# New order of issue in a fused attention and max-out FFN kernel: values and weights ahead of other loads, FFN units between attention steps

## The chip, the cores and the metric

The kernel runs on one core of a Trainium2 chip. The metric is device time in microseconds of one execution; lower is better. Five engines work side by side, each strictly in the order of its own instructions: TensorE (PE, with its weight loads PEld), VectorE (DVE), ScalarE (ACT), GpSimd (POOL) and SyncE (SP), which only issues transfers here. Sixteen DMA engines move the data; transfers issued by SP and ACT go through hardware queues, those issued by POOL, which also turn fp32 into fp16 on the way, through a software queue.

## The reference

Four batches, eight heads, 768 tokens, 64 numbers per head. Heads 0, 2 and 6 look at all earlier tokens, the others ("streaming") only at 4 first tokens and the last 64. The attention's output, 3072 rows of 512, goes through an FFN whose hidden layer is the maximum of three products.

```python
scores = scale * np.matmul(q, k.transpose(0, 1, 3, 2))
stream_keep = causal & (is_sink | in_win)
mask = np.where(retr[0, :, 0, 0, None, None], full_mask, stream_mask)
scores = np.where(mask[None, :, :, :], scores, -1000000000.0)
scores = scores - np.max(scores, axis=-1, keepdims=True)
a = np.exp(scores)
a = a / (np.sum(a, axis=-1, keepdims=True) + 1e-09)
attn = np.matmul(a, v)
x = np.ascontiguousarray(attn.transpose(0, 2, 1, 3)).reshape(B * S, H * D)
h = np.maximum(np.maximum(x @ w1, x @ w2), x @ w3)
return (h @ w_out).astype(np.float32)
```

Shapes: q, k, v are 4 x 8 x 768 x 64, w1 to w3 512 x 768, w_out 768 x 512, all fp32; the result is 3072 x 512 fp32. The kernel works in fp16 with sums in fp32.

## The kernel before

The function `fast` defines some forty small steps and runs them in the order of the list `PROGRAM` (line 83; the loop over it is at line 854). Each item is a step's name, its numbers and, where one applies, a letter for the engine (d DVE with copy, r DVE with a reduction as copy, a ACT, p POOL, s SP's queue). Nothing reorders afterwards: the list alone says what each engine and each queue does first, and an engine whose next instruction waits holds all behind it.

Work is cut by batch (0 to 3) and by half (tokens 0 to 383 and 384 to 767). Batch 0 is treated apart, since it must start at once: its q and k come pair of heads by pair of heads, are cast and turned on PE; later batches come whole by POOL's queue in fp16 and are turned on DVE. The steps that matter here:

- `hl half pair n` (`load_pairs`, line 206): SP loads k and q of batch 0, 192 KB for two heads. `cast`, `turnp`: cast to fp16 and turned by three PE transposes each for k and q. `kx0`: the far keys of streaming heads are copied out.
- `load_v b half` (line 292): SP loads the values, 768 KB a half; for batch 0 with 768-byte runs (three rows of 64 floats), for later batches in three parts with 256-byte runs. `vc half h0 n` casts four heads of them, `vt half blocks` (`sort_v`, line 507) sorts them by PE into rows, `y` and `v` fill the tables of values, `vx` and `va`, that attention reads.
- `load b quad which` (line 248): POOL issues k and q of a later batch, 768 KB of fp16 together, in runs of 24 rows of a head (3072 bytes). `turn` is a DVE transpose of a quarter; `kx` copies far keys.
- `w 0`, `w 1`, `w 2` (line 392): POOL issues a weight, 768 KB of fp16 in runs of 1536 bytes; `w 3` is w_out.
- `s0 half u pair` (line 589): scores of batch 0 and their exponential on ACT; `k0` the masks. `s b step` and `k` the same for later batches. Scores lie in two PSUM tiles (`sps`).
- `av b half hp` (line 711): attention times values for two heads, and DVE's division; its result `x` is turned by PE (`x b half hp`) or, with the letter D, by a transposing DMA from SP.
- `f b half wi ni` (`hidden`, line 449): a unit of the FFN, four matmuls of 384 columns with weight wi and block ni; wi 0 is copied out, 1 and 2 are folded in by DVE as a maximum. There are 18 units to a half; they and the outputs use four PSUM banks (`bkp`). `o b half tb`: an output tile of 128 rows, six matmuls of 512 columns, copied and written by SP.
- `gs wi` (`gate`, line 282): a two-element DMA from SP that reads a weight; SP's next transfer is issued only when that weight has landed. `gp` does the same on POOL for a pair of batch 0. `idle n`: n matmuls on zeros.

A staging tile of `hl` exists twice (`pairs2`), one of values three times (`stage`), so the third `hl` of the pairs waits for the casts of the first.

Of the kernel before, what the change touches and what calls it, by code (L numbers as in the profile page):

```python
# [96 lines left out]
    "turn 1 0 0 1, turn 1 0 1 0, turn 1 1 0 0, kx 1 0 p, y 0 1 5:8:2 r a, f 0 0 0 3 a, s0 1 1 3",
    "s0 1 1 2, f 0 0 0 0 a, f 0 0 0 4 a, f 0 0 0 5 a, f 0 0 0 2 a, gs 0, s0 1 0 2, turn 1 1 1 1",
    "turn 1 1 1 0, s0 1 2 2, f 0 0 0 1 a, y 0 1 4:5:1 r a, k0 1 1 2 p, turn 1 1 0 1",
    "k0 3 1 2 d, av 0 1 0 D, k0 2 0 1 d, av 0 1 1 D, k0 2 1 0 p, k0 2 0 0 p, s 1 1, k 1 1 X 0 d",  # L100
    "k0 2 1 1 p, k 1 1 X 1 d, av 0 1 2 D, load 2 0 0, f 0 0 1 4, f 0 0 1 5, f 0 0 1 3, s 1 0",
    "av 0 1 3, f 0 0 1 2, k 1 0 Y 0 d, f 0 0 1 0, kx 1 1 d, f 0 0 1 1, f 0 0 2 1, s 1 2",
    "k 1 2 Y 0 p, f 0 0 2 2, x 0 1 3 d, f 0 0 2 0, f 0 0 2 4, f 0 1 0 4 a, f 0 1 1 4, f 0 0 2 3",
    "turn 2 0 0 1, s 1 3, f 0 1 0 2 d, k 1 2 X 0 p, f 0 0 2 5, load_v 1 0 s, v 1 0 3 a",
    "turn 2 0 0 0, f 0 1 1 2, flags, w 3, load 2 0 1, k 1 2 X 1 d, y 1 0 1:8:2 r p, f 0 1 2 2, f 0 1 0 0 a, s 1 5",
    "y 1 0 4:5:1 s p, y 1 0 4:5:1 r p, f 0 1 1 0, f 0 1 2 0, y 1 0 1:8:2 s a, f 0 1 0 1 d, s 1 7",
    "f 0 1 0 3 d, k 1 1 Y 0 p, k 1 0 X 0 p, load_v 1 1 s, v 1 1 2 d",
    "k 1 0 X 1 d, v 1 0 1 p, f 0 1 1 1, f 0 1 2 1, f 0 1 2 4, f 0 1 1 3",
# [944 lines left out]
```

## Time and profile before

| | us |
|---|---|
| median of 3 runs | 190.82 |
| lowest, highest | 190.44, 192.43 |
| the profiled execution, its whole time | 190.84 |
| its span, first to last instruction | 189.3 |
| PE busy in the span | 178.8 |
| DVE, ACT, POOL busy | 139.4, 101.2, 82.7 |

The mean granted clock of TensorE over the span is 0.994. Matmuls overlap in the records, so a busy PE is not PE at its peak; idle time of an engine matters only where another engine or the end of the run waits for it. "Busy" in the line of DMA shares counts packets of all queues, so it can pass 1. A wait for several semaphores is put down to the one that came last. HBM was read for 25.17 MB, which is every input once, and written for 6.29 MB, the result.

### The profile page before, as it was taken

The numbers are of one execution on the slowest core, as the hardware profiler recorded it, in microseconds if no ns is written. First come the engines' busy times: TensorE is split into PE (matmuls) and PEld (weight loads), VectorE is DVE, ScalarE is ACT, GpSimd is POOL, SyncE is SP. The second block draws the span as 40 slices with busy tenths as digits, with TensorE's granted clock in tenths as the row PEclk, the third lists the DMA queues.
The fourth block names the chain that finished last, engine by engine and source line by source line (L and its number), as shares of the span: only waits on it lengthen the run. The fifth ranks groups of instructions, "written<-read, shape, count | busy, mean of one in ns | idle before, by whom it ended". The sixth has DMA issues, their size and how long they took to land.

```text
span 189.3 us, 4743 instructions
## 1 busy us (share of the span) xinstructions
PE 178.8 (94%) x1854; PEld 105.0 (55%) x1854; DVE 139.4 (74%) x297; ACT 101.2 (53%) x163; POOL 82.7 (44%) x146
## 2 busy tenths in 40 slices
PE   6888889899999999999999999999999999999990
PEld 2444545666556456755566455856665567455540
DVE  4366999986979999785889976874855768537721
ACT  4579989745695542957438556464555420331020
POOL 7775799704899961125953680205144000000000
PEclk9999999999999999999999999999999999999997
DMA  4999999999899999969989321131122032421043
GB/s 125 313 325 290 214 212 198 170 126 201 150 146 171 161 234 196 259 89 178 283 135 213 78 94 55 24 66 55 21 57 68 0 112 44 115 108 47 0 167 119
DMA packets 44105, 26.60 MB, mean 140 GB/s; under 512 B 31022, under 2 KB 39470, under 8 KB 44078
## 3 DMA queue, kind: packets, MB, share of 16 engines
q1 hardware_dynamic: 39614, 18.19, 40.3%
q0 software_dynamic: 4192, 7.87, 24.4%
q8 instruction: 15, 0.25, 0.5%
q10 hardware_dynamic: 272, 0.20, 0.3%
q14 instruction: 12, 0.10, 0.2%
HBM read 25.17 MB, written 6.29 MB: 166 GB/s over the span
## 4 chain that ended last, share of the span: by engine, by line
PE 79%; DMA 9%; POOL 5%; issue 2%; SPq 2%; DVE 1%; ACT 0%; ACTq 0%; POOLq 0%
PE yy L442 45%; PE yy L472 15%; PE st L682 7%; PE oacc L725 7%; DMA vs<-in_v_dram 6%; POOL pt L378 4%; PE yst L442 3%; DMA qs<-in_q_dram 2%; SPq L206 2%; PE yst L472 1%; POOL vn L505 1%; DVE kx L566 0%; POOL kx L578 0%; POOL qn L220 0%; POOL vx L532 0%
## 5 line engine op out<-in xcount | busy, mean ns | idle before, releaser
L378 POOL TENSOR_TENSOR pt<-pt,kb 128x256 f16<-128x256 f16 (+4 forms) x49 | 42.1, 883 | 43.6 <-ACT pt L699 43.2
L699 ACT ACTIVATE pt<-st 128x1024 f16<-128x1024 f32 (+2 forms) x51 | 43.5, 909 | 31.1 <-PE st L682 31.0
L442 PE MATMUL yy<-xT,w2t 128*128 128x384 f16 x180 | 36.0, 326 | 0.0
L442 PE MATMUL yy<-xT,w0t 128*128 128x384 f16 x184 | 35.0, 326 | 0.0
L442 PE MATMUL yy<-xT,w1t 128*128 128x384 f16 x176 | 34.7, 326 | 0.0
L472 PE MATMUL yy<-woutt,hT 128*128 128x512 f16 (+1 forms) x138 | 31.9, 372 | 0.0
L459 DVE TENSOR_TENSOR acc<-yy,acc 128x384 f16<-128x384 f32 x44 | 24.2, 554 | 9.7 <-PE yy L442 6.7
L459 DVE TENSOR_TENSOR hT<-yy,acc 128x384 f16<-128x384 f32 x45 | 24.8, 556 | 4.7 <-PE yy L442 2.8
L274 DVE STREAM_TRANSPOSE KQ<-kq 128x384 f32<-128x384 f32 x24 | 25.3, 1131 | 0.0
L442 PEld LDWEIGHTS <-w1t 128*128 128x128 f16 x192 | 18.1, 98 | 12.3 <-issue 0.4
L442 PEld LDWEIGHTS <-w0t 128*128 128x128 f16 x192 | 17.8, 98 | 12.8 <-issue 1.1
L442 PEld LDWEIGHTS <-w2t 128*128 128x128 f16 x192 | 17.9, 98 | 11.8 <-issue 0.2
L481 ACT COPY ot<-yy 128x512 f32<-128x512 f32 (+1 forms) x17 | 9.7, 568 | 26.9 <-PE yy L472 24.1
L455 ACT CAST acc<-yy 128x384 f16<-128x384 f32 x31 | 14.6, 491 | 17.1 <-PE yy L442 14.6
L472 PEld LDWEIGHTS <-hT 128*128 128x128 f16 x150 | 14.4, 98 | 14.9
L725 PEld LDWEIGHTS <-pt 128*128 128x128 f16 x472 | 17.0, 97 | 4.3 <-POOL pt L378 1.0
L725 PE MATMUL oacc<-va,pt 128*128 128x65 f16 x392 | 18.8, 193 | 0.0
L732 DVE TENSOR_TENSOR x<-oacc,sums 128x384 f16<-128x384 f32 x32 | 17.8, 557 | 1.1
L378 DVE TENSOR_TENSOR pt<-pt,kb 128x512 f16<-128x512 f16 (+5 forms) x35 | 15.1, 444 | 3.2 <-ACT pt L699 3.1
L637 ACT ACTIVATE pt<-st 128x1024 f16<-128x1024 f32 (+5 forms) x22 | 15.4, 760 | 1.2 <-PE st L616 1.2
L682 PE MATMUL st<-KQ 32*128 32x128 f16 (+2 forms) x342 | 14.9, 257 | 0.0
L725 PE MATMUL oacc<-vx,pt 128*128 128x65 f16 x80 | 11.9, 192 | 0.7 <-POOL pt L378 0.7
(115 smaller groups left out, 184.4 us busy)
## 6 DMA issues: line engine op xcount, KB each, us to landing
out_dram<-ot SPq DMA_DIRECT2D x24, 256.0 KB, 3.0
vs<-in_v_dram SPq DMA_DIRECT2D x18, 256.0 KB, 5.5
ks<-in_k_dram SPq DMA_DIRECT2D x8, 192.0 KB, 5.3
qs<-in_q_dram SPq DMA_DIRECT2D x7, 192.0 KB, 4.5
kq<-in_k_dram POOLq DMA_DIRECT2D x3, 384.0 KB, 6.3
kq<-in_q_dram POOLq DMA_DIRECT2D x3, 384.0 KB, 9.1
kq<-in_k_dram POOLq DMA_DIRECT2D x3, 288.0 KB, 4.8
kq<-in_q_dram POOLq DMA_DIRECT2D x3, 288.0 KB, 6.3
```

The source lines that it names most:

```text
L274: nc.vector.transpose(out=dst.rearrange("c (p j) -> c j p", j=n)[:, j0:j1], in_=src.rearrange("c (j i) -> c j i", i=R),)
L378: engine.tensor_tensor(out=x, in0=x, in1=of_blocks(kb, pattern, rows), op=ALU.mult)
L442: nc.tensor.matmul(begun_units[b, half, wi, ni][:, 0:HALF], w_t[wi][:, ks, ni * P : (ni + 1) * P], xT[b, half, ks].rearrange("p a t -> p ( ...
L455: op(out=acc[b, half, ni], in_=yy[:, 0:HALF])
L459: nc.vector.tensor_tensor(out=acc[b, half, ni] if wi == 1 else hT[b, half, ni], in0=yy[:, 0:HALF], in1=acc[b, half, ni], op=ALU.max,)
L472: nc.tensor.matmul(yo[:, 0:n], hT[b, half, ns][:, tb * P : (tb + 1) * P], woutt[:, ns, c : c + n], start=(ns == 0), stop=(ns == NNB - 1),)
L481: op(out=ot[:, c : c + n], in_=yo[:, 0:n])
L637: nc.scalar.activation(out=pts[0, half, hp, u][:, r0:r1, c0:c1], in_=sts[hp][:, r0:r1, c0:c1], func=AF.Exp, scale=sc,)
L682: nc.tensor.matmul(sts["XY"[g // 2]][:, g % 2, c0 : c0 + n * P], KQ[rows, 0, ki * P : (ki + 1) * P] if kind == "p" else kx[b % 2][quad][ro ...
L699: nc.scalar.activation(out=pts[b, s, xy][:, r0:r1, c0:c1], in_=st[:, r0:r1, c0:c1], func=AF.Exp, scale=sc,)
L725: nc.tensor.matmul(o[:, i, r, 0 : D + 1], at[b, h, kind, ki, qi], vv[:, 0 : D + 1], start=(n == 0), stop=(n == len(todo) - 1), skip_group_ ...
L732: nc.vector.tensor_tensor(out=x, in0=o[:, :, :, 0:D], in1=rc.unsqueeze(3).to_broadcast([P, HB, 2, D]), op=ALU.mult,)
```

## The change

The list `PROGRAM` is replaced as a whole. Apart from three single `idle 1` items that are dropped, and the engine letters of many copies and masks, it holds the same items; all functions are the same.

- SP's queue: the values of half 0 (`load_v 0 0`) come right behind half 0's q and k, ahead of `hl 1 0 2` and `hl 1 2 2`. The values of half 1 (`load_v 0 1`), which had no gate, come behind `gs 0`, with the transposes of half 1's x behind them. Then `load_v 1 0`, the three outputs of half 0, `load_v 2 0` and `load_v 1 1`.
- POOL's queue: `w 0`, `w 1`, `w 2`, then `load 1 0`, `w 3`, `load 1 1`; before it was `load 1 0`, `w 0`, `load 1 1`, `w 1`, `w 2`, and `w 3` later. `w 0` now stands behind the casts of half 0's values, both on POOL; between the weights lie fills and two casts of half 1's third pair.
- PE: half 0's values are sorted and its attention done with less of half 1 in between; half 0's units start ahead of most of half 1's scores, and half 1's scores, the sorting of its values (`vt 1`) and its attention lie between half 0's units. All 18 units of half 0, its three outputs and two units of half 1 come ahead of batch 1's first scores (`s 1 1`); before, six units did.
- `idle 7` and `idle 3` come together at the start. From the unit `f 3 0 1 4` on the order is that of before.

The old and the new list from their starts to a little behind `s 1 1`; the rest goes on in the same way:

```diff
@@ PROGRAM @@
-    "idle 7, cleark 0 p, hl 0 1 1 ss, hl 0 2 2 ss, cast 0 0 ad, turnp 0 0 da, idle 3, cast 0 1 pp",
-    "turnp 0 1 aa, hl 1 0 2 ss, cast 0 2 pp, s0 0 1 0, clear 0 p, s0 0 1 1, turnp 0 2 dd",
-    "kx0 0 2 d, clear 1 p, cleark 1 p, cast 0 3 ad, s0 0 0 0, kx0 0 1 r, s0 0 0 1, idle 1, cast 1 0 dp",
-    "turnp 1 0 da, load_v 0 0 0 4 s, vc 0 0 4 d, turnp 0 3 aa, load_v 0 0 4 4 s, vc 0 4 4 a",
-    "hl 1 2 2 ss, idle 1, kx0 0 3 r, s0 0 0 3, s0 1 1 0, cast 1 1 pp, load 1 0",
-    "cast 1 3 ap, turnp 1 1 a, w 0, vt 0 02 dd, cast 1 2 ad, y 0 0 1:4:2 s r, s0 0 1 2, gp 1 2, vt 0 1 d",
-    "k0 0 1 2 p, y 0 0 1:4:2 r r, s0 0 0 2, turnp 1 2 dd, y 0 0 4:5:1 s p, load_v 0 1 s, s0 1 0 0",
-    "kx0 1 2 r, av 0 0 0, y 0 0 5:8:2 s p, y 0 0 5:8:2 r p, kx0 1 1 r, turnp 1 3 da, s0 0 1 3",
-    "kx0 1 3 r, y 0 0 4:5:1 r a, load 1 1, w 1, gs 1, s0 1 0 1, av 0 0 3, av 0 0 1, vc 1 0 4 d",
-    "vc 1 4 4 p, x 0 0 0 a, s0 1 3 2, k0 1 0 2 p, x 0 0 3 a, turn 1 0 0 0, s0 1 3 0, k0 2 3 1 p",
-    "av 0 0 2, s0 1 0 3, gs 0, x 0 0 1 d, vt 1 02 ad, k0 3 0 2 p, vt 1 1 a, k0 0 3 2 p",
-    "k0 0 0 2 p, gs 0, x 0 0 2 d, s0 1 2 0, s0 1 1 1, idle 1, w 2, turn 1 0 1 1, y 0 1 1:4:2 r p",
-    "turn 1 0 0 1, turn 1 0 1 0, turn 1 1 0 0, kx 1 0 p, y 0 1 5:8:2 r a, f 0 0 0 3 a, s0 1 1 3",
-    "s0 1 1 2, f 0 0 0 0 a, f 0 0 0 4 a, f 0 0 0 5 a, f 0 0 0 2 a, gs 0, s0 1 0 2, turn 1 1 1 1",
-    "turn 1 1 1 0, s0 1 2 2, f 0 0 0 1 a, y 0 1 4:5:1 r a, k0 1 1 2 p, turn 1 1 0 1",
-    "k0 3 1 2 d, av 0 1 0 D, k0 2 0 1 d, av 0 1 1 D, k0 2 1 0 p, k0 2 0 0 p, s 1 1, k 1 1 X 0 d",
-    "k0 2 1 1 p, k 1 1 X 1 d, av 0 1 2 D, load 2 0 0, f 0 0 1 4, f 0 0 1 5, f 0 0 1 3, s 1 0",
-    "av 0 1 3, f 0 0 1 2, k 1 0 Y 0 d, f 0 0 1 0, kx 1 1 d, f 0 0 1 1, f 0 0 2 1, s 1 2",
-    "k 1 2 Y 0 p, f 0 0 2 2, x 0 1 3 d, f 0 0 2 0, f 0 0 2 4, f 0 1 0 4 a, f 0 1 1 4, f 0 0 2 3",
-    "turn 2 0 0 1, s 1 3, f 0 1 0 2 d, k 1 2 X 0 p, f 0 0 2 5, load_v 1 0 s, v 1 0 3 a",
-    "turn 2 0 0 0, f 0 1 1 2, flags, w 3, load 2 0 1, k 1 2 X 1 d, y 1 0 1:8:2 r p, f 0 1 2 2, f 0 1 0 0 a, s 1 5",
-    "y 1 0 4:5:1 s p, y 1 0 4:5:1 r p, f 0 1 1 0, f 0 1 2 0, y 1 0 1:8:2 s a, f 0 1 0 1 d, s 1 7",
-    "f 0 1 0 3 d, k 1 1 Y 0 p, k 1 0 X 0 p, load_v 1 1 s, v 1 1 2 d",
-    "k 1 0 X 1 d, v 1 0 1 p, f 0 1 1 1, f 0 1 2 1, f 0 1 2 4, f 0 1 1 3",
-    "v 1 1 3 a, v 1 0 0 a, v 1 0 2 p, av 1 0 2 D, k 1 3 X 0 p, k 1 5 X 0 p, s 1 4, av 1 0 3 D",
-    "av 1 0 1 D, load 2 1, k 1 7 Y 0 d, k 1 5 X 1 d, f 0 1 0 5 a, f 0 1 2 3, v 1 1 0 a",
...
+    "idle 3, idle 7, cast 0 0 dp, turnp 0 0 ad, cleark 0 d, s0 0 0 0, hl 0 1 1 ss, cast 0 1 pp",
+    "turnp 0 1 ad, hl 0 2 2 ss, cast 0 2 dp, cast 0 3 da, load_v 0 0 4 4 s, s0 0 1 0, vc 0 4 4 p",
+    "s0 0 1 1, clear 0 d, load_v 0 0 0 4 s, kx0 0 1 a, turnp 0 2 ad, kx0 0 2 a, turnp 0 3 dd, s0 0 0 1",
+    "kx0 0 3 r, vc 0 0 4 p, hl 1 0 2 ss, s0 0 0 2, cast 1 0 dd, vt 0 02 aa, w 0, vt 0 1 d",
+    "y 0 0 1:4:2 r d, s0 0 1 2, cast 1 1 aa, hl 1 2 2 ss, s0 0 0 3, y 0 0 5:8:2 s r, y 0 0 1:4:2 s p",
+    "av 0 0 1, av 0 0 0, w 1, y 0 0 4:5:1 r r, cast 1 2 pp, w 2, turnp 1 0 aa, y 0 0 4:5:1 s p, load 1 0",
+    "s0 0 1 3, turnp 1 1 aa, x 0 0 0 a, kx0 1 1 a, y 0 0 5:8:2 r r, cast 1 3 pd, av 0 0 3, s0 1 2 0",
+    "av 0 0 2, s0 1 0 1, x 0 0 1 d, turnp 1 3 ad, kx0 1 3 r, gs 0, x 0 0 3 d, x 0 0 2 d, flags, s0 1 1 0",
+    "k0 1 0 2 p, f 0 0 0 2 d, f 0 0 0 1 d, s0 1 3 0, k0 0 3 2 p, k0 0 1 2 d, s0 1 0 0, f 0 0 0 3 a",
+    "turnp 1 2 dd, kx0 1 2 r, f 0 0 0 4 d, w 3, s0 1 1 1, k0 1 1 2 d, s0 1 0 3, f 0 0 0 5 a, f 0 0 1 5",
+    "load 1 1, load_v 0 1 s, f 0 0 1 3, vc 1 0 4 a, f 0 0 0 0 d, f 0 0 1 0, k0 3 0 2 d, f 0 0 1 2",
+    "vc 1 4 4 p, k0 0 0 2 p, f 0 0 1 1, f 0 0 1 4, f 0 0 2 1, s0 1 2 2, s0 1 0 2, vt 1 02 aa",
+    "turn 1 0 0 0, turn 1 0 0 1, k0 2 0 1 p, vt 1 1 a, y 0 1 5:8:2 r a, turn 1 0 1 1, k0 2 0 0 p",
+    "y 0 1 4:5:1 r p, y 0 1 1:4:2 r a, f 0 0 2 0, s0 1 1 3, s0 1 1 2, f 0 0 2 2, k0 3 1 2 p, f 0 0 2 4",
+    "k0 2 1 0 p, av 0 1 0 D, av 0 1 1 D, f 0 0 2 5, av 0 1 2 D, clear 1 p, load_v 1 0 s, f 0 0 2 3",
+    "s0 1 3 2, o 0 0 2 a, load 2 0 1, k0 2 3 1 p, turn 1 0 1 0, k0 2 1 1 p, turn 1 1 0 0, av 0 1 3",
+    "turn 1 1 0 1, o 0 0 0 a, x 0 1 3 a, o 0 0 1 a, kx 1 0 p, f 0 1 0 4 a, load 2 0 0, turn 1 1 1 1",
+    "turn 1 1 1 0, kx 1 1 p, f 0 1 0 0 d, cleark 1 p, s 1 1, k 1 1 X 0 p, turn 2 0 1 1, k 1 1 X 1 p",
+    "y 1 0 4:5:1 s d, y 1 0 1:8:2 s d, f 0 1 0 1 d, f 0 1 1 1, f 0 1 0 3 d, k 1 1 Y 0 d, load_v 2 0 s",
...
```

80 rows, old and new, of the table PROGRAM are left out of this document.

## The prediction

> **What bounds the kernel now.** I read the page first (busy shares, the 40 slices, the queues), then the windows, then the chain of waits, and last the timelines of single engines.
>
> ```profile
> PE 178.8 (94%) x1854; PEld 105.0 (55%) x1854; DVE 139.4 (74%) x297; ACT 101.2 (53%) x163; POOL 82.7 (44%) x146
> PE   6888889899999999999999999999999999999990
> DMA  4999999999899999969989321131122032421043
> q1 hardware_dynamic: 39614, 18.19, 40.3%
> q0 software_dynamic: 4192, 7.87, 24.4%
> ```
>
> TensorE (PE) is full from about 36 us to the end; only the first seven or eight slices have holes, and in these the DMA engines are full. The windows (columns: busy time of PE, its weight loads, DVE, ACT, POOL, then clock, DMA share, GB/s) say the same:
>
> ```profile
> 0.00:5.00 5.00, 3.50 (x11) 1.17 (x12) 2.32 (x9) 2.00 (x3) 3.88 (x13) 1.00 0.48 124
> 5.00:10.00 5.00, 4.23 (x37) 2.22 (x36) 1.78 (x6) 2.73 (x7) 3.93 (x13) 1.00 1.04 324
> 10.00:15.00 5.00, 4.20 (x44) 2.16 (x44) 2.72 (x10) 4.19 (x7) 3.05 (x6) 1.00 1.10 326
> 16.00:18.00 2.00, 1.58 (x13) 0.71 (x11) 2.00 (x5) 2.00 (x5) 1.58 (x4) 1.00 1.11 280
> 18.00:20.00 2.00, 1.83 (x29) 1.29 (x31) 1.94 (x4) 2.00 (x5) 1.94 (x5) 1.00 1.08 225
> 20.00:22.00 2.00, 1.21 (x28) 0.81 (x27) 1.90 (x7) 1.66 (x5) 2.00 (x5) 1.00 1.10 217
> 24.00:26.00 2.00, 1.45 (x18) 0.67 (x15) 1.95 (x5) 1.68 (x3) 2.00 (x2) 1.00 1.15 214
> 40.00:50.00 10.00, 10.00 (x109) 6.04 (x108) 8.51 (x19) 5.64 (x8) 4.54 (x13) 1.00 1.25 183
> ```
>
> From 40 us on PE has no hole, so only the opening can be shortened, and work that moves within the full stretch buys nothing. The chain of waits gives the prices of PE's work and the long DMA; the other rows are PE's, POOL's, ACT's, DVE's and SP's timelines (start, duration, what):
>
> ```profile
> 11.51 12.11 DMA vs<-in_v_dram
> 66.83 7.80 PE yy L442 x48
> 62.30 2.59 PE yy L472 x12
> 119.51 1.30 PE oacc L725 x42
> ...
> 27.50 0.81 PE L442 MATMUL yy<-xT,w0t 128*128 128x384 f16 x4
> 34.72 0.40 PE L682 MATMUL st<-KQ 32*128 32x256 f16 x5
> 36.01 0.20 PE L725 MATMUL oacc<-vx,pt 128*128 128x65 f16 x1 [0.65 <-POOL pt L378]
> 11.31 0.34 PE L238 MATMUL tr<-ident,kn 128*128 128x128 f16 x3
> 26.84 0.39 PE L616 MATMUL st<-KQ 64*128 64x384 f16 x4
> 11.31 0.51 POOL L220 CAST kn<-ks 128x384 f16<-128x384 f32 x1
> 12.22 0.76 POOL L260 DMA_DIRECT2D kq<-in_k_dram  x1
> 12.98 0.55 POOL L260 DMA_DIRECT2D kq<-in_q_dram  x1
> 16.88 0.77 POOL L399 DMA_DIRECT2D w0t<-in_moe_w_dram  x1
> 23.74 1.15 POOL L505 CAST vn<-vs 128x768 f16<-128x768 f32 x1 [1.10 <-DMA vs<-in_v_dram]
> 30.65 0.82 POOL L399 DMA_DIRECT2D w2t<-in_moe_w_dram  x1
> 13.88 0.83 ACT L505 CAST vn<-vs 128x768 f16<-128x768 f32 x1 [0.60 <-DMA vs<-in_v_dram]
> 4.10 0.51 ACT L220 CAST kn<-ks 128x384 f16<-128x384 f32 x1 [1.04 <-DMA ks<-in_k_dram]
> 27.22 6.84 DVE L274 STREAM_TRANSPOSE KQ<-kq 128x384 f32<-128x384 f32 x7
> 1.05 0.46 SPq L206 DMA_DIRECT2D ks<-in_k_dram  x1
> 36.81 4.17 SPq L739 DMA_TRANSPOSE xT<-x  x3
> ...
> w0t<-in_moe_w_dram POOLq DMA_DIRECT2D x1, 768.0 KB, 9.1
> ```
>
> **A common point.** In both orders PE starts batch 1's first scores (s 1 1) after the opening; before, at 34.72 us. The matmuls are the same but for three single idle ones that go. So I count what stands ahead of s 1 1. A matmul of a hidden unit is 7.80/48 = 0.1625 us, a unit of four 0.65; an output tile is six of 2.59/12 = 0.216, so 1.3; a matmul of attention times values is 1.30/42 = 0.031. The new order puts these ahead of s 1 1 that stood behind it: the twelve w1 and w2 units of half 0 (7.8), its three outputs (3.9), two units of half 1 (1.3), 33 matmuls of av 0 1 2 and av 0 1 3 (1.0), one turn of x (0.2): 14.2. With the 0.65 that PE waited for POOL's masks (the 36.01 row), the old order would be there at 34.72 + 14.2 + 0.65 = 49.6. Whatever earlier or later than 49.6 the new order starts s 1 1 is the gain or the loss, as long as PE is full behind it.
>
> **Step 1, the values of half 0.** They go ahead of four loads of 192 KB (half 1's first two pairs), 0.79 MB, at 326 GB/s 2.4 us. Their second part was there when ACT began its cast at 13.88; now at 11.5, the first part 1.2 us sooner. Both casts move to POOL (1.15 each): the second ends at 12.65, and w0 is issued there instead of at 16.88.
>
> **Step 2, w0.** SP's and ACT's loads of half 0 and half 1 are 4.72 MB, 3.93 without half 1's values. The first three windows moved 0.62 + 1.62 + 1.63 = 3.87 MB, so these 3.93 are through at 15.2. Batch 1's load was issued at 12.22, but the total stays at the hardware queue's 326 until about 17, so POOL's packets come in when the queue ahead has nearly run out. I let w0 flow from 15.2: 0.79 MB at 214 GB/s is 3.7, landed with 0.5 for the signal at 19.4. Before it was 16.88 + 9.1 = 26.0.
>
> **Step 3, the first unit.** It was at 27.50. w0 is no longer what ends last. POOL has, after w0: a fill, the issue of w1, two casts of half 1's third pair (0.5 each; its q lands among the last of SP's, 17.8 beside w0), the issue of w2 (0.82), a fill, the issue of load 1 0 (0.76 + 0.55), then the cast of the fourth pair's k, at about 21.8. PE turns that pair ahead of two of half 0's x, then come scores, then the unit: about 23.0, 4.5 sooner.
>
> **Step 4, PE to the sort of half 1's values (vt 1).** 13 units (8.45), six scores of 0.3 to 0.4 (26.84 row) less what runs side by side, 1.8, one pair turned (two rows of three, 0.35), some 0.4 of waits: 34.0. w1 and w2 stand behind w0 on a queue that never runs dry and land near 24 and 28.5, ahead of their first uses at 28 and 33; ACT and DVE keep up (DVE about 16 us of work between 20 and 40). If everything else were there, s 1 1 would follow 13.5 later, at 47.5: a gain of 2.1. This is what hides nothing and costs nothing; what is late is next.
>
> **Step 5, the values of half 1.** SP used to issue them at 11.51 without a condition. Now they stand behind a gate DMA that waits for w0 to land: 19.4, issued by 20.2. The first load, issued at 1.05, could be cast at 4.10; less 0.6 for its 0.2 MB, a load needs some 2 us before its bytes come: about 22. Behind that wait on SP are only the transposes of half 1's x, not yet due. But the software queue is full from then to over 40 us: w1, w2, load 1 0, w_out, load 1 1, all issued early. What such company costs stands in the 11.51 row: 12.11 us for 0.79 MB. At 326 GB/s to 16, and by the mean of 280 until about 17.1, 4.55 of the 4.72 MB had moved; the remaining 0.17 took until 23.6, about 26 GB/s, beside 215 to 225 of total traffic. The page's counts give why: 18.19 MB in 39614 packets is 459 bytes each, 7.87 in 4192 is 1876. If each engine takes one packet from each queue in turn, bytes divide as packet sizes: a values packet is 768 bytes (3 rows of 64 floats), one of batch 1's keys 3072 (24 rows in fp16), one of a weight row 1536. So the values get a third of 217, 72, beside weights and a fifth, 43, beside keys. From 22: 0.93 MB of w1 and w2 are left, 6.4 us at 145, values 0.46; load 1 0, 4.5 us at 174, values 0.19; the last 0.13 beside w_out: 34.3, usable at 34.8. The bounds: alone on the engines 24.4, at 43 throughout 40.3. I take 34.8, the nearest to the row that shows the sharing. POOL's cast then ends at 36.0, and PE, which reached vt 1 at 34.0, stands 2.1 us. ACT and POOL, both in order, stand at these casts from about 29, so nothing of theirs is done in the wait.
>
> **Step 6, from there to s 1 1.** vt 1 (nine matmuls of 512 columns, six of them in pairs) 1.3, five units 3.25, three scores 0.9, 75 av matmuls 2.3, a turn 0.2, three outputs 3.9, two units 1.3: 13.15, and 0.3 of short waits: 49.6, where the old order stood. The gain of step 4 is spent. DVE's five transposes of batch 1 behind the last hidden unit (6.84/7 = 0.98 each) end at the same time.
>
> **Step 7, batch 1's values.** SP issues them behind three transposes of x (4.17 together), about 44.5 to 46.5; they are 256-byte packets, at about 225 GB/s alone:
>
> ```profile
> 46.00:48.00 2.00, 2.00 (x31) 1.16 (x28) 1.35 (x3) 0.60 (x2) 2.00 (x2) 1.00 1.32 225
> ```
>
> POOL's load 2 0 0 (3072-byte packets, 1.8 us) falls into them, and then they get 256/3328, 17 GB/s: landed at about 52. DVE, in order, wants them at 50.6 for its first two fills; the accumulations behind these free PE's four banks. I take 1.6 lost; the bounds are 0 and 3.
>
> **The sum.** 0 for the opening and 1.6 behind it. The profiled execution took 190.84 us against a span of 189.3 and a median of 190.82: 190.84 + 1.6 = 192.4. Its own range, with step 5 from 33 to 37 and step 7 from 0 to 3: 189.5 to 195.
>
> **Rivals.** *The values come in time.* If they are castable before 32.8 (34.0 less 1.15), PE doesn't stand and the gain is 2.1: 188.7, faster. For it: the 0.17 MB is a small tail, and half the bytes each (107 GB/s) would land them at 29.3. Against it: every window from 18 to 26 us stays at the software queue's rate. Chance 0.24.
>
> *The clock falls.* A stand longer than the clock tolerates makes matmuls slow afterwards. The end of the run shows it:
>
> ```profile
> 186.00:188.00 2.00, 0.00 (x0) 0.00 (x0) 0.00 (x0) 0.00 (x0) 0.00 (x0) 0.80 0.49 168
> 184.59 0.35 PE yy L472 x6
> 1.50 3.17 PE L325 MATMUL idl<-zero 128*128 128x512 f16 x7 [1.50 <-DVE warm L328]
> ```
>
> A mean of 0.80 with half clock at the end is a fall at 187.2, 2.3 us after the last matmul at 184.9; cold, a 512-column matmul takes 3.17/7 = 0.45 us against 0.216. If the stand at vt 1 reaches 2.3, some 3.5 us at half speed cost 1.7: 194.1. Step 5's 2.1 lies just under it. Chance 0.16. The Trainium skill (TensorE: Matmul & The Clock Gate, the part on the HAM clock gate) lets the clock fall after at least one idle window of about 3.4 us; by that rule a stand of 2.1 is safe and the sum stays at 192.4, while the row at the end shows a fall after 2.3.
>
> *The weights don't come sooner.* Batch 1's load needed from 12.22 to about 17 before it moved a byte. If w0 needs over 8 us from issue, it lands after 23, units and gate both slip, and the run is about 3 longer: 195.4, the change not doing what it says. Chance 0.10; main case 0.50.
>
> **Range and chances.** 1% (1.9 us) is about what a measurement here can tell from no change. Below 188.9 lies half of the first rival and a little of the main case: 0.20. Above 192.7 lie some 0.4 of the main case and nearly all of the last two: 0.45. The rest 0.35. The range 188.2 to 196.0 takes in all four cases.
>
> **What would show it.** Right: w0's first unit at 22 to 24; POOL and ACT idle until a DMA of vs at 33 to 37; a PE hole of 1.5 to 4 us ahead of vt 1; s 1 1 at 48.5 to 51.5; a DVE wait for vs near 51. Wrong: the values there before 32.8, s 1 1 at 47.5 or sooner, or holes of PE after 60 us, which I have not looked for one by one in the new order.

## The result and the profile after

| us | before | after |
|---|---|---|
| median of 4 runs each, on one chip | 190.89 | 200.71 |
| lowest, highest | 190.44, 192.43 | 198.07, 202.14 |
| the profiled execution, its whole time | 190.84 | 202.14 |
| its span | 189.3 | 200.6 |
| PE busy | 178.8 | 182.8 |

The ratio is 1.046, with a 95% interval of 1.036 to 1.057: slower, and outside the predicted range of 188.2 to 196.0. The profiled execution is the slowest of the four, 1.4 us above their median. The mean clock of the four is 0.971 to 0.982 against 0.994 before; times the span, that is an estimated 7 us at half clock in the quickest and 10 to 12 in the others. So clock was lost in all of them; where it was lost is known for the profiled one alone. The page of after, its span, busy shares, slices of the clock and the chain by engine:

```profile
span 200.6 us, 4734 instructions
PE 182.8 (91%) x1851; PEld 105.7 (53%) x1851; DVE 145.1 (72%) x304; ACT 97.7 (49%) x159; POOL 82.9 (41%) x144
PEclk9988999969979999999999999999999999999999
PE 64%; DMA 25%; DVE 4%; SPq 2%; issue 1%; POOL 1%; ACT 0%; ACTq 0%
```

Three places of the clock's row lie under 9, a quarter of the chain that ended last is DMA, and the span grew by 11.3 us. PE idles 200.6 - 182.8 = 17.8 us of it, against 10.5 before: 7.3. It is also busy 4.0 us longer although it runs three matmuls fewer. Those are two different losses. Where PE stood, from the waits of PE in after (who waited for what, us in total, times, longest):

```profile
PE vb L508 <- POOL vn L500: 4.1, 1, 4.1
PE yy L437 <- DMA xT<-x: 3.6, 3, 2.4
PE tr L233 <- ACT qn L215: 1.6, 1, 1.6
```

Three stands, then: at the sort of half 1's values (vt 1), at the first units that need half 1's x, and in the opening at a cast of q. The transfers behind them, from the chain of waits (start, us, what):

```profile
14.06 7.98 DMA w0t<-in_moe_w_dram
22.82 15.75 DMA vs<-in_v_dram
50.15 5.79 DMA xT<-x
```

And the timelines of ACT, SP and PE around them, with the idle time ahead of an instruction and what ended it in brackets:

```profile
10.93 0.51 ACT L215 CAST qn<-qs 128x384 f16<-128x384 f32 x1 [1.98 <-DMA qs<-in_q_dram]
22.05 0.73 SPq L280 DMA_DIRECT2D gates<-w0t  x1
24.39 0.32 PE L437 MATMUL yy<-xT,w0t 128*128 128x384 f16 x1
39.50 2.15 PE L508 MATMUL vb<-vn,every 64*128 64x512 f16 x9 [4.12 <-POOL vn L500]
55.98 1.14 PE L437 MATMUL yy<-xT,w0t 128*128 128x384 f16 x6 [2.40 <-DMA xT<-x]
57.05 0.40 PE L677 MATMUL st<-KQ 32*128 32x256 f16 x5
```

The last row is s 1 1, 7.45 us behind the 49.6 at which the prediction put it. The second loss, busy time without more work, is the clock. The windows of after (busy time of PE, PEld, DVE, ACT, POOL, then clock, DMA share, GB/s), cut where the clock changes:

```profile
9.65:13.06 3.41, 1.64 (x16) 0.69 (x14) 1.90 (x7) 2.10 (x7) 0.83 (x1) 1.00 1.07 330
13.06:16.47 3.41, 3.27 (x17) 1.20 (x16) 1.11 (x2) 2.92 (x6) 1.95 (x3) 0.50 0.94 220
33.54:36.95 3.41, 1.84 (x17) 0.92 (x14) 3.38 (x6) 0.00 (x0) 0.00 (x0) 1.00 1.17 230
36.95:40.37 3.42, 0.87 (x7) 0.36 (x8) 1.43 (x2) 1.77 (x3) 1.45 (x2) 1.00 1.18 214
40.37:43.78 3.41, 3.41 (x16) 1.23 (x15) 0.56 (x1) 3.10 (x7) 1.82 (x3) 0.50 0.60 118
54.02:57.43 3.41, 1.45 (x23) 0.84 (x23) 0.76 (x2) 0.48 (x1) 0.28 (x1) 1.00 1.07 223
57.43:60.85 3.42, 3.42 (x23) 1.59 (x12) 2.83 (x6) 1.94 (x2) 1.91 (x2) 0.50 1.08 306
```

Each of the three stands is followed by a stretch of 3.41 us at half clock. In a stretch in which PE has work throughout, half of its time is lost: 3.41/2, an estimate of 1.7 us at most.

Why the values took 15.75 us is in the DMA queues of after between 32 and 36 us (packets, MB, share of 16 engines), while both queues had work:

```profile
q0 software_dynamic: 421, 0.55, 77.1%
q1 hardware_dynamic: 425, 0.33, 33.0%
```

The software queue moved 421 packets and the hardware queue 425, one for one, and the bytes stand as the sizes of the packets: 425 of 768 bytes are 0.33 MB. Single microseconds say the same for each size on the software queue: 98 packets of 1536 bytes beside 100 from 27 to 28 us, 54 (all but one of 3072 bytes) beside 54 from 32 to 33, 128 of 1024 bytes (w_out's rows) beside 128 from 35 to 36. The values' own rate is 0.33/4 = 82 GB/s; alone, the hardware queue moved 324 to 326 GB/s in before between 5 and 15 us, in packets of the same size. The first of the values' packets started at 26.4 us, 3.6 after the issue at 22.82; from then on they flowed for 11.7.

### The profile page after: what moved, and what is told of

The parts are those of the page before. It is cut to its first block, busy times and chain, and to the rows that moved or that the text cites. A ratio compares the mean times of both kernels' runs of the same rounds, so it can differ in the third digit from the quotient of the medians.

```text
span 200.6 us, 4734 instructions
## 1 busy us (share of the span) xinstructions
PE 182.8 (91%) x1851; PEld 105.7 (53%) x1851; DVE 145.1 (72%) x304; ACT 97.7 (49%) x159; POOL 82.9 (41%) x144
## 4 chain that ended last, share of the span: by engine, by line
PE 64%; DMA 25%; DVE 4%; SPq 2%; issue 1%; POOL 1%; ACT 0%; ACTq 0%
PE yy L437 36%; DMA vs<-in_v_dram 12%; PE yy L467 11%; DMA xT<-x 9%; PE oacc L720 6%; PE st L677 5%; DMA w0t<-in_moe_w_dram 4%; PE yst L437 3%; SPq L201 2%; DVE KQ L269 1%; DVE pt L373 1%; PE yst L467 1%; PE vb L508 1%; POOL vn L500 1%; DVE acc L454 1%
## 5 line engine op out<-in xcount | busy, mean ns | idle before, releaser
L373 POOL TENSOR_TENSOR pt<-pt,kb 128x512 f16<-128x512 f16 (+5 forms) x49 | 43.5, 905 | 40.9 <-ACT pt L694 34.0
L437 PE MATMUL yy<-xT,w0t 128*128 128x384 f16 x184 | 37.0, 332 | 3.7 <-DMA xT<-x 3.6
L437 PE MATMUL yy<-xT,w1t 128*128 128x384 f16 x176 | 35.4, 331 | 0.0
L476 ACT COPY ot<-yy 128x512 f32<-128x512 f32 (+1 forms) x15 | 8.5, 568 | 30.8 <-PE yy L467 29.0
L450 ACT CAST acc<-yy 128x384 f16<-128x384 f32 x26 | 12.1, 482 | 17.7 <-PE yy L437 16.6
L720 PEld LDWEIGHTS <-pt 128*128 128x128 f16 x472 | 17.5, 97 | 4.7 <-DVE pt L373 0.7
L727 DVE TENSOR_TENSOR x<-oacc,sums 128x384 f16<-128x384 f32 x32 | 17.8, 558 | 1.1
L373 DVE TENSOR_TENSOR pt<-pt,kb 128x256 f16<-128x256 f16 (+5 forms) x35 | 16.1, 473 | 3.0 <-ACT pt L694 3.0
L677 PE MATMUL st<-KQ 32*128 32x128 f16 (+2 forms) x342 | 15.2, 258 | 0.0
L450 DVE CAST acc<-yy 128x384 f16<-128x384 f32 x20 | 10.9, 554 | 5.6 <-PE yy L437 5.2
```

The lines of the kernel that those rows point to most:

```text
L373: engine.tensor_tensor(out=x, in0=x, in1=of_blocks(kb, pattern, rows), op=ALU.mult)
L437: nc.tensor.matmul(begun_units[b, half, wi, ni][:, 0:HALF], w_t[wi][:, ks, ni * P : (ni + 1) * P], xT[b, half, ks].rearrange("p a t -> p ( ...
L450: op(out=acc[b, half, ni], in_=yy[:, 0:HALF])
L476: op(out=ot[:, c : c + n], in_=yo[:, 0:n])
L677: nc.tensor.matmul(sts["XY"[g // 2]][:, g % 2, c0 : c0 + n * P], KQ[rows, 0, ki * P : (ki + 1) * P] if kind == "p" else kx[b % 2][quad][ro ...
L720: nc.tensor.matmul(o[:, i, r, 0 : D + 1], at[b, h, kind, ki, qi], vv[:, 0 : D + 1], start=(n == 0), stop=(n == len(todo) - 1), skip_group_ ...
```

## The experiments

The theory (A in the expectations): half 1's values are late because they start behind the gate and then share packet by packet with a software queue that is always full; the stand at vt 1 and the half clock behind it are most of the loss. The rivals are named with each run. Edits are to the list of the changed kernel unless the text says otherwise; a diff of the list shows the items around an edit.

**Values without the gate.**

```diff
-hl 1 2 2 ss, s0 0 0 3
+hl 1 2 2 ss, load_v 0 1 s, s0 0 0 3
-load 1 1, load_v 0 1 s, f 0 0 1 3
+load 1 1, f 0 0 1 3
```

> The changed order, with the load of half 1's values put on SP's queue right behind half 1's last q and k, ahead of the gate that waits for w0. Theory A (the gate and the sharing with the software queue make the values late, and that costs the stand before vt 1 and the clock behind it): they land by 25 us instead of 38.6, PE's hole of 4.1 us ahead of vt 1 and the half clock from 40.4 to 43.8 go, w0 lands up to 2.4 us later; batch 1's first scores start at 51 to 53 instead of 57.1, and the run takes 194 to 197. Theory B (the new order loses its time elsewhere: in the transposes of x and in the later order): the values are early, but the run stays within 2 us of 200.7. Theory C (the clock alone): as B, with some 2 us gained.

195.1 us (193.18 to 195.83), 1.023 [1.015, 1.031] of before. The chain of this run, and then PE's timeline:

```profile
12.73 10.71 DMA w0t<-in_moe_w_dram
```

```profile
23.49 2.74 PE L437 MATMUL yy<-xT,w0t 128*128 128x384 f16 x8 [2.13 <-DMA w0t<-in_moe_w_dram]
36.60 0.38 PE L508 MATMUL vb<-vn,every 64*128 64x512 f16 x1
52.25 0.40 PE L677 MATMUL st<-KQ 32*128 32x256 f16 x5
```

The sort starts without a wait, and s 1 1 comes 4.8 us earlier. But w0 now needs 10.71 us instead of 7.98, PE stands 2.13 us for it, and the clock was half from 22.70 to 29.53. The gate did protect w0; it cost more than it saved. The ratio to before falls from 1.046 to 1.023: about half of the loss goes with it.

**The same gate in the order of before.** One item added to the kernel before, where POOL's queue and everything else stay:

```diff
-y 0 0 4:5:1 s p, load_v 0 1 s, s0 1 0 0
+y 0 0 4:5:1 s p, gs 0, load_v 0 1 s, s0 1 0 0
```

> The order before with one gate on w0 put ahead of the load of half 1's values on SP, nothing else changed. Theory A: w0 lands at about 25 (a little sooner, without the values' tail), the values are issued then, share with load 1 1, w1 and w2, and land at 37 to 42 instead of 23.6; vt 1 and half 1's attention wait, PE gets a hole of 8 us or more before 45, less what it makes up, and the run takes 197 to 205. Theory B: the values' lateness costs less than 3 us: 191 to 194.

204.3 us (203.84 to 205.74), 1.076 [1.071, 1.082]. The chain, and then PE's timeline:

```profile
26.39 9.23 DMA vs<-in_v_dram
```

```profile
36.94 2.86 PE L513 MATMUL vb<-vn,every 64*128 64x512 f16 x9 [11.89 <-POOL vn L505]
47.90 0.40 PE L682 MATMUL st<-KQ 32*128 32x256 f16 x5
```

A gate on these values alone makes the old order 7.6% slower. Here it is the late issue that costs, at 26.39 instead of 11.51, and not the sharing: the transfer took 9.23 us, less than the 12.11 of before, and from 32 to 34 us the software queue moved only 35 packets beside 762. PE stands 11.89 us, and the clock is half for the 13.65 us from 27.03 to 40.68, four stretches of 3.41 in a row. s 1 1 goes from 34.72 to 47.90.

**Idle matmuls in the stand.** Sixteen matmuls on zeros ahead of vt 1, so that the clock might stay up while the values come.

```diff
-s0 1 2 2, s0 1 0 2, vt 1 02 aa
+s0 1 2 2, s0 1 0 2, idle 16, vt 1 02 aa
```

> The changed order with sixteen idle matmuls on zeros (16 x 0.216 = 3.5 us) ahead of vt 1, where PE stands 4.1 us; everything else waits as long as before. Theory A with the clock as its second part: the clock stays full at 40 us, the matmuls of the 3.4 us behind the stand run at full speed, and the run is about 1.7 us shorter than the changed kernel: 198.5 to 199.5. If the clock has no part: no change, or up to 0.5 us longer by the idle matmuls that are still in flight.

198.4 us (196.85 to 200.65), 1.047 [1.038, 1.055]: by the ratio not told apart from the change. The fillers covered only the front of the stand; 2.02 us of it stayed, and the clock fell at 38.68 all the same. So this run does not price the clock by itself; it does show a fall behind a stand of 2.02 us.

**Half 1's x turned by PE.** Three pairs of half 1's x are turned by PE and copied by ACT instead of by DMA.

```diff
-av 0 1 0 D, av 0 1 1 D, f 0 0 2 5, av 0 1 2 D, clear 1 p
+av 0 1 0, av 0 1 1, f 0 0 2 5, av 0 1 2, x 0 1 0 a, x 0 1 1 a, clear 1 p
-s0 1 3 2, o 0 0 2 a, load 2 0 1
+s0 1 3 2, o 0 0 2 a, x 0 1 2 a, load 2 0 1
```

> The changed order with half 1's first three x turned on PE (nine small matmuls, 0.5 us, and three ACT copies) instead of by SP's transposing DMAs. Theory B, and theory A for its later part: the hole of 2.4 us at 56.0 goes, with it the half clock from 57.4 to 60.9 (1.7 us), and the run is 3 to 4 us shorter than the changed kernel: 196.5 to 198. If the half 1 units only wait for something else in its place (batch 1's keys, a bank): within 1 us of 200.7.

198.0 us (197.44 to 198.52), 1.040 [1.035, 1.044], near the number that was expected, but not by what was expected. The stand for xT ahead of s 1 1 is gone, but with nothing left between them on SP, batch 1's values were issued from 22.95 on, right behind half 1's, which shared with them:

```profile
39.10 2.86 PE L508 MATMUL vb<-vn,every 64*128 64x512 f16 x9 [5.66 <-POOL vn L500]
55.17 0.40 PE L677 MATMUL st<-KQ 32*128 32x256 f16 x5
```

The stand at vt 1 grew from 4.12 to 5.66, with two half-clock stretches (36.63 to 43.46), and ate most of the gain. An item that is taken off a queue lets what stands behind it go earlier.

**The same bytes in large packets.** The gate and the place stay, but SP's load reads heads 0 to 3 of batch 0 whole, in runs of 6144 bytes, in place of half 1's values; half 1 of batch 0 is computed from other values.

```diff
+        if (b, half) == (0, 1):
+            engine.dma_start(
+                out=vs.rearrange("p h j d -> p (h j d)"),
+                in_=v[0, 0 : H // 2].rearrange("h (p r) d -> (h p) (r d)", p=32),
+            )
+            return
         if b == 0 and half in sorted_halves:
```

> The changed order with the same gate and the same 768 KB on SP's queue, but in runs of 6144 bytes instead of 768: in place of half 1's values of all heads it loads heads 0 to 3 of batch 0 whole, so half 1 of batch 0 is computed from other values. Theory A (one packet of each queue in turn, so bytes divide as packet sizes): 6144 against 1536 gives the values most of the traffic, they land 5 to 8 us after issue instead of 15.75, at 28 to 31, no hole ahead of vt 1, no half clock at 40, w 1 and w 2 some 3 us later, s 1 1 at 51 to 53, time 194 to 197. Rival (the hardware queue is served behind the full software queue, or bytes are shared equally): 10 to 16 us from issue to landing as with small runs, the hole stays at 2 us or more, time 198 or more.

194.4 us (191.82 to 195.11; before beside it 191.08). The queues of this run between 26 and 28 us, and then PE at the sort:

```profile
q1 hardware_dynamic: 90, 0.55, 69.4%
q0 software_dynamic: 94, 0.14, 39.0%
```

```profile
32.48 0.38 PE L514 MATMUL vb<-vn,every 64*128 64x512 f16 x1
```

90 packets against 94, one for one again, and now the hardware queue has four fifths of the bytes. No wait at the sort. This tells the theory from a hardware queue that is served last, or from equal bytes: only the size of a packet was changed. What PE still stands for ahead of s 1 1 is half 1's x, 0.65 and 1.52 us, with a half clock from 47.97 to 51.38.

**Values on the software queue.** No sharing at all: POOL loads half 1's values, cast on the way, between w 1 and w 2; SP's load and the casts go.

```diff
-av 0 0 1, av 0 0 0, w 1, y 0 0 4:5:1 r r, cast 1 2 pp, w 2
+av 0 0 1, av 0 0 0, w 1, lvc 1 0 8, y 0 0 4:5:1 r r, cast 1 2 pp, w 2
-load 1 1, load_v 0 1 s, f 0 0 1 3, vc 1 0 4 a, f 0 0 0 0 d, f 0 0 1 0, k0 3 0 2 d, f 0 0 1 2
-vc 1 4 4 p, k0 0 0 2 p, f 0 0 1 1
+load 1 1, f 0 0 1 3, f 0 0 0 0 d, f 0 0 1 0, k0 3 0 2 d, f 0 0 1 2
+k0 0 0 2 p, f 0 0 1 1
```

> The changed order, but half 1's values go through the software queue, cast on the way, between w 1 and w 2; SP's load of them and POOL's and ACT's casts go. Theory A (sharing packet by packet made the values late; the stand at vt 1 and the half clock behind it are most of the loss): in one queue nothing is shared, the values need some 3.6 us of the queue and land at 29 to 31, no hole ahead of vt 1, no half clock at 40; w 2 lands 3.6 later at 34 or so; the stand for the transposes of x stays (the loads of batch 2 are as before), s 1 1 at 51 to 53, time 194 to 197. Rival (the values only hid something else, such as late weights or a new order that is longer in itself): the hole moves to another wait, s 1 1 stays at 55 or later, time 198 or more.

192.5 us (191.11 to 194.67), 1.009 [1.005, 1.014]. The transfer, issued at 15.67 (KB as written, us to landing), then PE at the sort and ahead of s 1 1, then the window in which it stood:

```profile
vn<-in_v_dram POOLq DMA_DIRECT2D x1, 384.0 KB, 11.6
```

```profile
32.34 0.38 PE L508 MATMUL vb<-vn,every 64*128 64x512 f16 x1
45.92 0.52 PE L437 MATMUL yy<-xT,w0t 128*128 128x384 f16 x2 [1.06 <-DMA xT<-x]
47.22 1.14 PE L437 MATMUL yy<-xT,w0t 128*128 128x384 f16 x6 [0.79 <-DMA xT<-x]
48.29 0.29 PE L677 MATMUL st<-KQ 32*128 32x256 f16 x4
```

```profile
44.99:48.40 3.41, 1.69 (x12) 0.81 (x16) 0.99 (x3) 0.98 (x2) 0.78 (x2) 1.00 1.10 224
```

The values are there at 27.3, better than expected; the stand at vt 1 and its half clock are gone, and with them about four fifths of the loss (1.046 to 1.009). It is better than expected in another point, too: the opening kept its full clock, the first unit came at 21.7, and the two stands for x, 1.85 us together, left the window 1.69 us busy and the clock up.

**That, and x by PE.** As above, with the x of half 1 turned by PE as in the fourth run, and a gate on w 2 ahead of batch 1's values, so that they stay late.

```diff
-av 0 1 0 D, av 0 1 1 D, f 0 0 2 5, av 0 1 2 D, clear 1 p, load_v 1 0 s, f 0 0 2 3
+av 0 1 0, av 0 1 1, f 0 0 2 5, av 0 1 2, x 0 1 0 a, x 0 1 1 a, clear 1 p, gs 2, load_v 1 0 s, f 0 0 2 3
-s0 1 3 2, o 0 0 2 a, load 2 0 1
+s0 1 3 2, o 0 0 2 a, x 0 1 2 a, load 2 0 1
```

> The same, and half 1's x of the first three pairs is turned by PE and copied by ACT instead of by a transposing DMA; the values of batch 1 stand behind a gate on w 2. Theory A: both stands are gone, s 1 1 at 49 to 51, where the old order stands (49.6), time 191.5 to 194.5; what is left over 190.5 is the holes behind s 1 1 and an opening half clock where it comes. Rival (the new order is longer in itself): s 1 1 at 52 or later with no hole over 1 us ahead of it, time 196 or more.

189.7 us (189.4 to 190.56), 0.993 [0.990, 0.997]: a little faster than before, the only run of which that can be said. s 1 1 in PE's timeline, and the emptiest window of the opening:

```profile
46.82 0.40 PE L677 MATMUL st<-KQ 32*128 32x256 f16 x5
```

```profile
10.16:13.57 3.41, 2.17 (x22) 1.01 (x21) 1.97 (x6) 3.18 (x8) 2.20 (x3) 1.00 1.10 337
```

That is better than expected, too. The new order is not long in itself. With values and x in time s 1 1 stands at 46.8, close to the 47.5 that the prediction gave for "if everything else were there".

**Fillers in the opening.** The run before, with `idle 7` ahead of the turning of half 0's last pair and `idle 8` ahead of the first unit.

```diff
-kx0 0 2 a, turnp 0 3 dd
+kx0 0 2 a, idle 7, turnp 0 3 dd
-k0 1 0 2 p, f 0 0 0 2 d
+k0 1 0 2 p, idle 8, f 0 0 0 2 d
```

> The same as the one before, and idle matmuls where PE waits in the opening: seven ahead of the turning of half 0's last pair, eight ahead of the first unit of the FFN. If the opening's holes cost clock: no half clock ahead of 187, and 1 to 3 us less than the one before, 190 to 192. If the clock in the opening costs nothing because the loads bound it: the same within 0.7 us, or up to 1 us more where the idle matmuls delay work.

192.3 us (191.4 to 194.78), 1.007 [1.002, 1.012], a miss: 2.6 us more than without them, where at most 1 was expected. Neither profile has a half clock ahead of the end, so the fillers had nothing to protect in them, and they are not free: PE's busy time rose from 178.3 to 180.7, and s 1 1 came at 48.6.

**x by DMA without company.** The run with values on the software queue and x turned by DMA, but with batch 2's first loads behind s 1 1 and their turns later.

```diff
-s0 1 3 2, o 0 0 2 a, load 2 0 1, k0 2 3 1 p
+s0 1 3 2, o 0 0 2 a, k0 2 3 1 p
-f 0 1 0 4 a, load 2 0 0, turn 1 1 1 1
+f 0 1 0 4 a, turn 1 1 1 1
-s 1 1, k 1 1 X 0 p, turn 2 0 1 1, k 1 1 X 1 p
+s 1 1, k 1 1 X 0 p, load 2 0 0, load 2 0 1, k 1 1 X 1 p
-turn 2 0 0 1, f 0 1 1 4, s 1 2
+f 0 1 1 4, s 1 2
-f 0 1 2 4, s 1 7, k 1 0 X 0 p
+f 0 1 2 4, turn 2 0 0 1, turn 2 0 1 1, s 1 7, k 1 0 X 0 p
```

> The changed order with half 1's values on the software queue (as in e5), half 1's x turned by DMA as in the change, but batch 2's first loads (load 2 0 1, load 2 0 0) issued only behind s 1 1, and their DVE turns later. If the transposing DMAs are late because of the key packets beside them (in e5 issue to landing 7.8 us for the first, PE stood 1.06 and 0.79 us): they land 3 to 5 us after issue, no hole over 0.5 us between 44 and 48, s 1 1 at 46.5 to 47.5 against 48.29. If a transposing DMA is as slow by itself: landing, holes and s 1 1 as in e5. The whole time says less, since batch 2's keys are later: 190 to 193.

194.4 us (192.77 to 197.51), 1.018 [1.011, 1.025]. The three transposing DMAs, median from issue to landing, in the run with company (first row) and in this one, then the sort and s 1 1 in PE's timeline of this one:

```profile
xT<-x SPq DMA_TRANSPOSE x3, 7.2
```

```profile
xT<-x SPq DMA_TRANSPOSE x3, 2.8
```

```profile
34.56 0.38 PE L508 MATMUL vb<-vn,every 64*128 64x512 f16 x1
48.32 0.29 PE L677 MATMUL st<-KQ 32*128 32x256 f16 x4
```

2.8 us against 7.2, and no stand for x: from the sort to s 1 1 13.76 us against 15.95. So the key packets of the next loads make these transfers late. s 1 1 itself is where it was, since in this execution the opening had a stand of 2.06 us and a half clock behind it and the sort began 2.2 us later. Behind s 1 1 PE stood 3.05 us, until 62.70, for a mask on DVE, and the clock was half from 61.75 to 68.58. DVE did not wait for a load between 50 and 64 us; it was busy, with another mask that took 3.93 us (0.80 in the run with company, why is open) and, right ahead of the mask that PE needed, with the two turns that were moved (2.07 us). The profiled execution took 197.51 us, the others 192.77 to 194.91; how much of this they had is not known, so the whole time says nothing of the transposes.

**Two attempts to go below 189.7.** The x of the first pair of batch 1's half 1 by PE, too; and, in a second kernel, also av 1 0 1 behind s 1 3.

```diff
-av 1 1 0 D, v 2 0 0 a, s 2 7, o 0 1 1 d, f 1 0 2 0, k 2 1 Y 0 p
+av 1 1 0, v 2 0 0 a, s 2 7, o 0 1 1 d, f 1 0 2 0, x 1 1 0 a, k 2 1 Y 0 p
```

```diff
-v 1 0 1 p, av 1 0 1 D, v 1 0 2 p
-s 1 3, av 1 0 2 D
+v 1 0 1 p, v 1 0 2 p
+s 1 3, av 1 0 1 D, av 1 0 2 D
```

> e6 and the x of the first pair of batch 1's half 1 turned by PE, too: the hole of 0.78 us at 108.2 in e6, which waited for that transposing DMA, goes, and 0.2 us of PE's work comes: 189.0 to 189.5, 0.4 to 0.7 under e6's 189.72. If the hole passes to the next thing that is late: the same as e6.

> e10 with av 1 0 1 behind s 1 3, so that DVE's mask has PE's scores as cover: the hole of 0.61 us at 57.7 goes: 188.5 to 189, some 0.5 under e10. If s 1 3 has to wait for ACT's exponential there: no gain, or 0.3 us of loss.

191.1 us (189.2 to 193.43), 1.002 [0.998, 1.006], and 190.0 (189.17 to 191.03), 0.998 [0.995, 1.001]; both misses. In the first the stand of 0.78 shrank to 0.32 and the span is 188.5, but the profiled execution took 190.10 us and others up to 193.43. In the second the stand for the mask went, one of 0.51 came at 65.9, and the one for a transposing DMA was 0.98 at 108.4: the next late thing takes its place. Both kernels hold the edits of the run with 189.7, and neither is told apart from before, so the 0.7% of that run was not found again.

**Values on the software queue in the old order.** The kernel before, with `lvc 1 0 8` ahead of `load 1 0` and SP's load and the casts taken out.

```diff
-cast 1 1 pp, load 1 0
+cast 1 1 pp, lvc 1 0 8, load 1 0
-y 0 0 4:5:1 s p, load_v 0 1 s, s0 1 0 0
+y 0 0 4:5:1 s p, s0 1 0 0
-av 0 0 1, vc 1 0 4 d
-vc 1 4 4 p, x 0 0 0 a
+av 0 0 1
+x 0 0 0 a
```

> The order of before with half 1's values on the software queue, cast on the way, ahead of batch 1's first load. If e6's 189.7 comes from the path of the values alone, this is as fast or faster (188.5 to 190). If it comes from the order with the path: no gain here, since in the order of before the values cost PE 0.40 us at vt 1 and w 0 lands later behind them: 190.5 to 193.

189.7 us (189.28 to 190.55), 0.997 [0.994, 1.000]: not told apart from before, and the same 189.7 as the best run of the new order. The two were not run side by side. So the gain of 0.7% is not shown to come from the order; the old one may reach it by the path of the values alone.

## Why the prediction was wrong

**Steps 1 and 2** put w0's issue at 12.65 and its landing at 19.4; it was 14.06 and 22.0. The first 1.4 us are step 1's: the values of half 0 were to land at 11.5, 2.4 sooner than before, since four loads no longer stood ahead of them. From the chain of after, what w0's issue waited for:

```profile
5.48 7.75 DMA vs<-in_v_dram
13.28 0.77 POOL vn L500
```

They landed at 13.23. The loads of this opening were late as a whole: ACT's cast of the last pair's q waited for its DMA until 10.93, PE stood 1.62 us, and a half clock followed. In the run with values on the software queue the opening had no half clock; there the values landed at 11.93 and w0 was issued at 12.76. The other 1.2 us are w0's transfer, 7.98 where 6.75 had been worked out: it was to flow at 214 GB/s from 15.2, but all queues together moved 146 GB/s from 15 to 16 us, 72 from 16 to 17, and only then 190 and more.

**Steps 3 and 4** held. The first unit, at 23.0, came at 24.4, late by as much as w0's issue; the sort was reached at 39.50 - 4.12 = 35.4 instead of 34.0, again by those 1.4. With a full clock in the opening it was 21.7 to 21.9 and 32.3 to 32.6.

**Step 5 is where this lateness became a stand: its mechanism was right, its size was not.** The shares came out: 72 GB/s beside weights and 43 beside keys were worked out, and 100 packets of 768 bytes from 27 to 28 us are 77, 54 from 32 to 33 are 41. From issue to use 14.6 us were predicted and 15.75 measured; the bytes flowed for 11.7 instead of 12.3, but the wait ahead of the first one was 3.6 instead of 1.8. And the issue hangs on w0 through the gate, so the 2.6 us of steps 1 and 2 passed through it whole, and PE stood 4.12 us instead of 2.1. (One sum in this step is off, without effect on the time: its own rates give 4.50 MB by 17.1 us, not 4.55, so the tail was 0.22 MB and some 34 GB/s, not 0.17 and 26.) The two bounds of the range treated the end of the transfer as uncertain and its start as known.

**The clock was a case beside the others, with a chance of 0.16, and should have been a part of the main one.** It was read from the end of the run as a threshold of 2.3 us on a stand. The stretch of before that ends with this fall, and the windows of after, say something else:

```profile
183.77:187.19 3.42, 1.16 (x12) 0.71 (x9) 1.14 (x2) 0.27 (x1) 0.00 (x0) 1.00 0.64 231
```

What counts is how much of one fixed stretch of 3.41 us PE is idle; the last matmul of before ended 2.3 us ahead of the fall, but the stretch had begun 3.4 ahead of it, with PE busy for 1.16. In after the clock fell at 13.06, 40.37 and 57.43; the distances, 27.31 and 17.06, are 8 and 5 times 3.41. It fell behind stretches in which PE was busy 1.64, 0.87 and 1.45 us, and did not behind 1.84, nor behind 1.69 and 2.17 in two of the experiments. So a stand of 1.6 us can be enough where other small holes lie in the same stretch, as in the opening of after, and it depends on where the stretches lie whether a stand of 2.1 is. The 2.1 forecast for vt 1 was inside the danger, not just under it. The prediction had weighed the Trainium skill (TensorE: Matmul & The Clock Gate, the part on the HAM clock gate), which lets the clock fall after at least one idle window of 3.4 us: here stretches half empty were enough, so the measurement decides against that reading. The same part says that the window is 4096 cycles, 3413 ns, and free-running; with that the trace agrees, by the distances above.

**Step 6** put s 1 1 13.6 us behind the sort's start. Measured are 17.55: 2.40 of them the stand for half 1's x, some 1.5 the half clock. Without both it is 13.76 (x by DMA without company) and 14.26 (with three turns more on PE). The work had been counted right; that transposes of x on SP wait beside batch 2's keys had not been priced. The prediction named them as standing behind the gate, "not yet due", and looked at the values behind them in step 7 instead. Those were late as well, and POOL waited 9.3 us for them, but PE never did: **step 7**'s 1.6 was put down to the wrong transfer.

**The sum**, in spans: 200.6 against the predicted 189.3 + 1.6 = 190.9, so 9.7 to explain. vt 1 starts 3.5 late (39.50 against 36.0), from there to s 1 1 17.55 - 13.6 = 3.95 more: 7.45. The rest, 2.3, lies behind s 1 1, on top of the 1.6 that step 7 had put there: the third half clock, 57.43 to 60.85, and small stands. The sum had 0 up to s 1 1 and 1.6 behind it; in the profiled execution it was 7.45 and 3.9. In the prediction's own terms, the stand at vt 1 was sized at half of what it was, the stand for half 1's x in step 6 was put at nothing, and the clock was left out of the main case. The price of a stretch can be read from PE's busy time for the same 1851 matmuls. The pages of the run with values on the software queue, with no half clock ahead of the end, and of the run with large packets, with one stretch:

```profile
PE 178.4 (94%) x1851; PEld 104.9 (55%) x1851; DVE 144.6 (76%) x304; ACT 96.6 (51%) x158; POOL 83.3 (44%) x144
```

```profile
PE 179.9 (93%) x1851; PEld 105.2 (55%) x1851; DVE 143.8 (75%) x304; ACT 97.4 (51%) x159; POOL 83.0 (43%) x144
```

178.4 with none, 179.9 with one, 182.8 in after with three: about 1.5 us each. It is less where PE stands in part of the stretch: 180.5 with two in the run without the gate, 182.0 with three in the run of x without company, 1.1 and 1.2 each.

**What was right to fear and what was not.** The rival "the weights don't come sooner" needed over 8 us from w0's issue to its landing and was nearly met (7.98). "The values come in time" fell to the packet shares. No case joined two stands, and none went past 195.4.

## What to carry to other kernels

Where a transfer on a hardware queue starts beside a software queue that never runs dry, work out its time by packets, one for one, not by bytes; if its runs are short, put it on the full queue at the place where it is due. A gate passes on every delay of what it waits for, and what was hidden by an early issue is then paid by all that stand behind it. Price a stand of PE by the fixed stretches of 3.41 us that it half empties, and count the 1.1 to 1.5 us that each cost here with the main case, not as a case of its own.

## What the runs showed of the hardware

- While both queues have work, their packets alternate one for one whatever their size: 425 of 768 bytes beside 421, nearly all of 1024 or 3072, and 90 of 6144 bytes beside 94 of 1536. In the tail of a transfer the counts part: in before from 18 to 23 us it was 215 beside 444.
- The clock changes only at multiples of 3.41 us from one another, in each of the kept traces, and falls behind a stretch in which PE is idle for about half: in these traces it fell behind every stretch at full clock with 1.64 us busy or less, and stayed behind those with 1.69 or more. One stretch was an exception: without the gate, 2.00 us of busy time made of many small matmuls, and a fall:

```profile
19.29:22.70 3.41, 2.00 (x32) 1.24 (x28) 2.60 (x8) 3.27 (x5) 2.81 (x16) 1.00 1.16 211
22.70:26.11 3.41, 2.62 (x8) 1.04 (x8) 0.56 (x1) 0.00 (x0) 1.15 (x1) 0.50 1.16 209
```

- While transposing DMAs ran beside key loads, the whole traffic sank, though the engines' share stayed over 1. In the run with values on the software queue:

```profile
38.00:40.00 2.00, 1.96 (x22) 1.03 (x21) 1.93 (x7) 0.00 (x0) 1.46 (x5) 1.00 1.07 208
42.00:44.00 2.00, 2.00 (x16) 0.99 (x13) 1.95 (x5) 0.64 (x3) 0.72 (x3) 1.00 1.41 70
44.00:46.00 2.00, 0.94 (x5) 0.28 (x4) 1.98 (x3) 0.99 (x3) 1.64 (x4) 1.00 1.21 220
```

With the same key loads and x turned by PE the second of these windows moved 239 GB/s. Whether the transpose itself or its place among the packets does it was not tried.
